# Block transposes on VectorE for the last seven head pairs, and another order of scores and masks in the first batch

## The chip, the core and the metric

The kernel runs on one core of one Trainium2 chip. The engines of a core run side by side, each through its own queue in order: TensorE (PE, matmuls and transposes by an identity), VectorE (DVE), ScalarE (ACT), GpSimd (POOL) and SyncE (SP, which here only issues DMAs). The metric is the device time in microseconds of one launch, the median of several runs.

## What is computed

Two blocks follow each other: block-sparse attention over 4 batches, 8 heads, 768 positions and a head size of 64, and then a Fourier mixing block with a two-layer network over rows of 512.

```python
scores = scale * np.matmul(q, k.transpose(0, 1, 3, 2))
# mask: block window, first and last block, three sampled blocks of 32 per block row
scores = np.where(mask, scores, -1000000000.0)
attn = np.exp(scores - np.max(scores, axis=-1, keepdims=True))
attn = attn / (np.sum(attn, axis=-1, keepdims=True) + 1e-09)
x = np.matmul(attn, v).transpose(0, 2, 1, 3).reshape(B, S, H * D)

u = x + np.real(np.fft.fft(np.fft.fft(x, axis=1), axis=2))
un = (u - mean(u)) / np.sqrt(var(u) + 1e-06)
return u + np.maximum(un @ w_ch1, 0.0) @ w_ch2
```

## The kernel before

Two heads make a pair, and there are 16 pairs, numbered n, four to a batch. A pair needs q and k with the head's 64 features along the partitions: `turned[n, 0]` (qT) and `turned[n, 1]` (kT), each 128 partitions (two heads of 64) by 768 positions. The positions of q are not in their natural order but in the one that the Fourier part wants (`_ORDER`); those of k stand six to a partition of the load, so that a tile of 128 keys holds every sixth position.

`load_q` and `load_k` bring q and k in by DMA with positions on the partitions, in pieces of 256 bytes. `turn(n, a, half)` (L433 to L464) turns one half: three or four TensorE transposes of 128 by 128 into a PSUM bank (L447), then for k one ScalarE copy (L450), for q nine small copies in all (L456) that put the positions in order. After the second half a ScalarE square with a running sum (L462) keeps a bound on the scores, which at the end decides whether a slower general path (`general`) has to run; with these inputs it does not.

The main loop is `slot(sl)` (L1177). A slot is two units, and a unit is 128 keys by 384 queries of both heads; six slots make a pair, 24 a batch or phase, and 96 all of it. In a slot come the scores of its two units (`scores`, L470), their exp (`weigh`, L488), then the products with v of the slot before (`values`, L512). In phase 0 the mask is added to the scores by TensorE, as a second, bf16 product of two small matrices of 24 rows (`of_k`, `off_q`, L483), and the exp goes straight to the tile `e`; row sums are matmuls as well (`add_up`, L569). From phase 1 on, VectorE multiplies the exp by a mask of bytes (L499), and GpSimd adds up the sums (L509). Score banks in PSUM are two, one for each unit of a slot.

In between stands work that a planner places: it keeps, while the program is built, a model of when each engine will be free (`busy`, `when`, `free`). Short things wait in the list `short`: a turn of the next pair, `place` (L532, transposes the attention's output back, "xt" in the profile), `total` (L575), `mask_step` (L317). `gap` issues what the model says is ready. At the end of a slot a loop (L1238) issues what is left. Turns of pair n + 1 are put on the list in slots 1, 2 (q) and 4, 5 (k) of pair n; pairs 9 to 15 are turned while pairs 8 to 14 are worked on, in phases 2 and 3. The mixing block of a batch (`mixer`: the Fourier products, `quad` with line L898 and L903, `channels` with L954 and L957) runs in the phases after its own, as steps of the list `late` between attention slots, and for the last batch after the loop.

Also in phase 0, 32 chunks of the two weight matrices, which come as pairs of 32-bit words, are rounded to fp32 (`w_round`, L404): two ScalarE and five VectorE operations a chunk, 1.42 chunks a slot. `w_load` fills six rooms for them.

Before the loop, `turn(0, 1, 0)` and `turn(0, 0, 0)` turn the first halves of pair 0, `warm` issues matmuls whose result is not used, and VectorE builds the mask's matrices (`spread_k`, `spread_q`, `twice`). For the first turn of q the copies alternate between VectorE and ScalarE.

Of the kernel before, what the change touches and what calls it, by code (L numbers as in the profile page):

```python
# [11 lines left out]
FP32 = mybir.dt.float32  # L12
# [6 lines left out]
ACT = mybir.ActivationFunctionType  # L19
# [45 lines left out]
           ((384, 64, 191, 64, 64, -1), (704, -128, 64, 63, 63, -1), (640, 127, 0, 1, 1, 1)))  # L65


def _rows(view, tile):

    got = []  # L70
    for t, p0, runs, jump, n, s0, step in _ORDER:
        if t != tile:
            continue
        at = view[s0:s0 + 1, :]
        row, col = list(at.ap[0])[0], list(at.ap[1])
        if jump > 0:
            got.append((p0, runs * n, bass.AP(tensor=at.tensor, offset=at.offset,
                                              ap=[[jump * row, runs], [step * row, n], col])))
            continue
        for r in range(runs):  # L80
            at = view[s0 + r * jump:s0 + r * jump + 1, :]
            got.append((p0 + r * n, n, bass.AP(tensor=at.tensor, offset=at.offset,
                                               ap=[[step * row, n], col])))
    return got
# [3 lines left out]
def kernel(  # L88
# [14 lines left out]
    nc = tc.nc  # L103

    B, H, S, D = q.shape
    DM = H * D
    FF = w_ch1.shape[1]
    P = 128
    C = S // P
    BLK = 32  # L110
    NB = S // BLK
    NR = sampled_blocks.shape[1]
    HS = S // 2
# [7 lines left out]
    scale = 1.0 / float(D) ** 0.5  # L121
    KA = D + NB
    NP = H // 2
    LIMIT = 400.0

    const = ctx.enter_context(tc.tile_pool(name="const", bufs=1))

# [25 lines left out]
    peaks = const.tile([P, 2 * B * NP], FP32, name="peaks")  # L153

    ld = ctx.enter_context(tc.tile_pool(name="ld", bufs=1))
    ldv = ctx.enter_context(tc.tile_pool(name="ldv", bufs=2))
    tp_p = ctx.enter_context(tc.tile_pool(name="tp_p", bufs=2))
# [9 lines left out]
    ps_s = ctx.enter_context(tc.tile_pool(name="ps_s", bufs=2, space=PSUM))  # L167
# [6 lines left out]
    when = {"PE": 0.0, "ACT": 0.0, "DVE": 0.0, "POOL": 0.0}  # L174
    free = {"m": [0.0, 0.0], "t": [0.0]}

    def busy(engine, us, after=0.0):
        when[engine] = max(when[engine], after) + us
        return when[engine]
# [11 lines left out]
    HOP = 0.1  # L191

    pairs = [(b, j) for b in range(B) for j in range(NP)]
    loaded, v_of = {}, {}

    def load_k(n, queue=None):

        b, j = pairs[n]
        kt = loaded.get((n, 1))
        if kt is None:  # L200
            kt = ld.tile([P, C, 2, D], FP32, tag="k", name="kr")
        for i in range(2):
            (queue or nc.sync).dma_start(out=kt[:, :, i, :],
                                         in_=k[b, 2 * j + i].rearrange("(p c) d -> p c d", p=P))
        loaded[n, 1] = kt

    def load_q(n):

        b, j = pairs[n]
        qt = loaded.get((n, 0))  # L210
        if qt is None:
            qt = loaded[n, 0] = ld.tile([P, T, 2, 2, D], FP32, tag="q", name="qr")
        for t in range(T):
            for i in range(2):
                rows = q[b, 2 * j + i][2 * P * t:2 * P * (t + 1), :]
                nc.sync.dma_start(out=qt[:, t, :, i, :],
                                  in_=rows.rearrange("(p r) d -> p r d", r=2))
# [36 lines left out]
    def bit(n):  # L254
# [5 lines left out]
                      in_=bass.AP(tensor=_words(sampled_blocks, NB * NR), offset=0,  # L260
                                  ap=[[0, NB], [1, 2 * NB * NR]]))
# [3 lines left out]
    def warm(n):  # L265

        m = ps_m.tile([P, P], FP32, tag="m", name="warm")
        for _ in range(n):
            nc.tensor.matmul(m, ident, ident, start=True, stop=True)
# [4 lines left out]
                         func=ACT.Exp)  # L274
# [15 lines left out]
    at_k = acc_p.tile([P, 2, 2 * HS], BF16, tag="acc", name="at_k")  # L290
    at_q = acc_p.tile([P, 2, 2 * HS], BF16, tag="acc", name="at_q")
    of_k, off_q, keep_q = at_k[:, 0, :], at_q[:, 0, :], at_q[:, 1, :]

    def twice(t):
        nc.vector.tensor_copy(out=t[D:D + NB, :], in_=t[0:NB, :])
# [3 lines left out]
    kb = bit(1)  # L299
# [86 lines left out]
    for w, w_sb in ((w_ch1, w1_sb), (w_ch2, w2_sb)):  # L386
        rows, cols = w.shape
        words = _words(w, rows * cols)
        for row in range(rows // P):
            for col in range(0, cols, WN):  # L390
                src = bass.AP(tensor=words, offset=2 * (row * P * cols + col),
                              ap=[[2 * cols, P], [1, 2 * WN]])
# [37 lines left out]
    turned, e_of, acc_of, o_of, sums_of, x_of, sp_of = {}, {}, {}, {}, {}, {}, {}  # L430
    s_at, e_at, oT_at, acc_at = {}, {}, {}, {}

    def turn(n, a, half):  # L433

        t = loaded[n, a]
        if half == 0:
            turned[n, a] = tp_p.tile([P, S], FP32, tag="qk"[a] + "T", name="qk"[a] + "T")
        dst = turned[n, a]
        first = n == 0 and half == 0
        tag, pool = ("m", ps_m) if first and a == 0 else ("t", ps_t)  # L440
        tp, at = pool.tile([P, 512], FP32, tag=tag, name="tp"), bank(tag)
        if a == 0:
            parts = [t[:, c // 2, c % 2, :, :] for c in (range(4, 6) if half else range(4))]
        else:
            parts = [t[:, T * half + c, :, :] for c in range(T)]
        for c, part in enumerate(parts):
            nc.tensor.transpose(tp[:, c * P:(c + 1) * P], part, ident)  # L447
        done = busy("PE", 0.15 * len(parts)) + HOP
        if a == 1:
            nc.scalar.copy(out=dst[:, half * HS:(half + 1) * HS], in_=tp[:, 0:HS])  # L450
            give(at, busy("ACT", 0.5, done))
        else:
            for i, (to, to_jump, frm, jump, cnt, step) in enumerate(_TURNED[half]):
                on, copy = (("DVE", nc.vector.tensor_copy) if n == 0 and (half == 1 or i % 2 == 0)
                            else ("ACT", nc.scalar.copy))
                copy(out=_grid(dst, to, 2, to_jump, cnt, 1),  # L456
                     in_=_grid(tp, frm, 2, jump, cnt, step))
                end = busy(on, 0.27 if cnt > 1 else 0.18, done)
            give(at, end)
        if half == 1:  # L460
            flat = t.rearrange("p t r i d -> p (t r i d)" if a == 0 else "p c i d -> p (c i d)")
            nc.scalar.activation(out=flat, in_=flat, func=ACT.Square,  # L462
                                 accum_out=peaks[:, 2 * n + a:2 * n + a + 1])
            busy("ACT", 1.05)  # L464

    UP = 2 * C
    UNITS = len(pairs) * UP
    SLOT = 2

    def scores(u):  # L470
        n, w = divmod(u, UP)
        half, c = divmod(w, C)
        qT, kT = turned[n, 0], turned[n, 1]
        s = ps_s.tile([P, 2, 512], FP32, tag="s", name="s")
        busy("PE", 0.72 if n >= NP else 1.0, max(e_at.get(u - SLOT, 0.0), z_at[u % 2]))
        s_at[u] = when["PE"] + HOP
        for i in range(2):
            nc.tensor.matmul(s[:, i, 0:HS], kT[D * i:D * i + D, c * P:(c + 1) * P],  # L478
                             qT[D * i:D * i + D, half * HS:(half + 1) * HS],
                             start=True, stop=n >= NP)  # L480
        if n < NP:
            for i in range(2):
                nc.tensor.matmul(s[:, i, 0:HS], of_k[D * i:D * i + NB, c * P:(c + 1) * P],  # L483
                                 off_q[D * i:D * i + NB, half * HS:(half + 1) * HS],
                                 start=False, stop=True)
        return s

    def weigh(u, s):  # L488
        n, w = divmod(u, UP)
        half, c = divmod(w, C)  # L490
# [313 lines left out]
    z_at = [0.0, 0.0]  # L804
# [287 lines left out]
    LEAVES = 9.0  # L1092
    SP = UP // SLOT
    SB = SP * NP
    W_PACE = 1.42
    short, apart, late = deque(), deque(), deque()
# [80 lines left out]
    def slot(sl):  # L1177
        phase, r = divmod(sl, SB)
        n, s = divmod(sl, SP)
        units = range(SLOT * sl, SLOT * sl + SLOT)  # L1180
        if sl < B * SB:
            for u, ps in [(u, scores(u)) for u in units]:
                weigh(u, ps)
        if not late:
            gap(1.5)
# [10 lines left out]
        if sl > 0 and s == (5 if reuse else 3) and sl <= B * SB:  # L1196
            b, j = pairs[n]
            at = oT_at[n, 0]
            if reuse:
                until(lambda: (b - 2, 0) in finished)  # L1200
                at = when["PE"] + LEAVES
# [3 lines left out]
        if sl < B * SB and n % NP == 1 and s == 1:  # L1205
            b = pairs[n - 1][0]
            at = oT_at[n - 1, 1]
            if b >= 2:
                until(lambda: (b - 2, 1) in finished)
                at = when["PE"] + LEAVES  # L1210
# [1 line left out]
        if sl > SB and s == 0 and sl <= B * SB:  # L1212
            short.append(("t", acc_at[n - 1, 1], lambda: total(n - 1)))
        if n + 1 < len(pairs):
            for at, a, half in ((1, 0, 0), (2, 0, 1), (4, 1, 0), (5, 1, 1)):
                if s == at:
                    short.append(("t", 0.0, lambda a=a, half=half: turn(n + 1, a, half)))
            if s == 1:
                load_v(n + 1)
# [9 lines left out]
        us = sum(step[1] for step in late)  # L1229
# [5 lines left out]
            channel_step()  # L1235
            gap(max(state["owed"], 0.0))

        while short and (s in (2, 5) or len(short) > 1 or phase == 0 or sl == B * SB):  # L1238
            short.popleft()[2]()
        if s == 3 and n + 2 < len(pairs):  # L1240
            load_q(n + 2)
        if s == 0 and 0 < n < len(pairs) - 1:
# [6 lines left out]
    def highest():  # L1249
# [7 lines left out]
        flag = sm.tile([1, 1], I32, tag="flag", name="flag")  # L1257
        nc.vector.tensor_scalar(out=flag, in0=top, scalar1=LIMIT, scalar2=None, op0=ALU.is_gt)
        return flag
# [9 lines left out]
    state["got"] = 2  # L1269
    turn(0, 1, 0)  # L1270
    turn(0, 0, 0)
    warm(3)
    spread_q(keep_q[0:NB, :], keep)
    w_loads()
    for sl in range(B * SB + 1):
# [112 lines left out]
```

## Time and profile before

| what | before |
|---|---|
| median of 11 runs | 1109.5 us (1108.31 to 1113.95) |
| the profiled execution | 1109.49 us, of which the span of its instructions is 1107.7 us |
| VectorE busy | 663.9 us, 60% of the span |
| transposes for q and k on TensorE (L447) | 192, of them 84 for pairs 9 to 15 |
| scores (L478), all records | 160.3 us busy |
| mask products of phase 0 (L483) | 96 records, 16.1 us busy |
| clock granted to TensorE, mean | 0.994 of full |

The profile is one execution on the chip. An operation is named by its line, its output and inputs and their sizes. A TensorE matmul in fp32 shows as two records, and matmuls are pipelined: the time from one start to the next is what a matmul costs its queue, and the duration of a record is longer than that. The attention's slots of phase 0 lie from 9.2 to 133 us, those of phase 1 to 248, phase 2 to 574, and phase 3 to about 825; then the last batch is mixed to the end.

### The profile page before, as it was taken

To read this page: it belongs to the slowest core of one execution; us is meant where nothing else is said; L and a number is where in the kernel's file an instruction comes from. 1 tells how busy PE (TensorE), PEld (TensorE's weight loads), DVE (VectorE), ACT (ScalarE), POOL (GpSimd) and SP (SyncE) were. 2 spreads that over 40 slices of the span, in tenths; PEclk is the share of its full clock that TensorE was granted. 3 is DMA by queue.
4 is the path that set the end of the run, shared out by engine and by line. 5 is a ranking of instruction groups with operands and counts; after the bars stand their busy time and mean duration, and the time that the engine had idled before them with its cause. 6 is when DMAs were issued, how large, how long until landed. Compare 5 with 4: busy or idle time off the path is not lost.

```text
span 1107.7 us, 12468 instructions
## 1 busy us (share of the span) xinstructions
PE 1067.3 (96%) x4446; PEld 545.2 (49%) x4446; DVE 663.9 (60%) x1216; ACT 393.5 (36%) x818; POOL 274.0 (25%) x302
## 2 busy tenths in 40 slices
PE   8999988998899999999999999999999999999996
PEld 4333333544455545444444555454444555568675
DVE  5888878497754525653458355544356446575563
ACT  6788755555112102253443212244330202120210
POOL 1000078688100001255537000344440001000000
PEclk9999999999999999999999999999999999999998
DMA  7756311011000000210110000211000000100001
GB/s 219 209 176 214 95 45 49 15 45 43 0 1 1 0 1 24 63 40 18 43 29 15 1 0 1 52 49 29 1 1 0 1 1 20 38 1 1 1 16 44
DMA packets 65187, 44.30 MB, mean 40 GB/s; under 512 B 52814, under 2 KB 57948, under 8 KB 65116
## 3 DMA queue, kind: packets, MB, share of 16 engines
q1 hardware_dynamic: 63228, 42.62, 13.7%
q10 hardware_dynamic: 1856, 0.79, 0.3%
q8 instruction: 37, 0.61, 0.2%
q14 instruction: 34, 0.28, 0.1%
q0 software_dynamic: 32, 0.01, 0.0%
HBM read 37.11 MB, written 6.29 MB: 39 GB/s over the span
## 4 chain that ended last, share of the span: by engine, by line
PE 87%; DVE 8%; ACT 3%; issue 2%; POOL 0%; ACTq 0%; DVEq 0%; POOLq 0%
PE y L954 23%; PE z L898 15%; PE s L478 11%; PE o L522 9%; PE yp L898 7%; PE yy L1017 6%; PE xp L898 4%; DVE e L499 2%; PE tp L447 2%; PE zp L711 1%; PE sp L569 1%; PE xt L540 1%; PE zp L682 1%; PE s L483 1%; PE utp L823 1%
## 5 line engine op out<-in xcount | busy, mean ns | idle before, releaser
L509 POOL TENSOR_TENSOR acc<-acc,e 128x384 f32<-128x384 f32 x192 | 198.2, 1065 | 91.5 <-DVE e L499 91.0
L499 DVE TENSOR_TENSOR e<-s,mask 128x768 f32<-128x768 f32 x144 | 131.0, 950 | 77.2 <-ACT s L497 76.8
L478 PE MATMUL s<-qT,kT 64*128 64x384 f32 x768 | 160.3, 522 | 7.6 <-DVE e L499 7.1
L522 PE MATMUL o<-e,vr 128*64 128x384 f32 x768 | 145.8, 501 | 0.0
L497 ACT ACTIVATE s<-s 128x768 f32<-128x768 f32 x144 | 109.2, 795 | 63.5 <-PE s L478 60.5
L957 DVE TENSOR_TENSOR x<-y,x 128x512 f32<-128x512 f32 x72 | 49.7, 690 | 134.0 <-PE y L954 133.9
L954 PE MATMUL y<-w_sb,hB 128*128 128x512 f32 x288 | 128.4, 595 | 1.1 <-DVE x L957 1.0
L954 PE MATMUL y<-w_sb,hA 128*128 128x512 f32 x288 | 128.8, 594 | 0.6 <-ACT zs L713 0.6
L509 POOL TENSOR_TENSOR acc<-e 128x384 f32<-128x384 f32 x48 | 51.7, 1098 | 228.9 <-DVE e L499 173.5
L903 DVE TENSOR_TENSOR hA<-z,hA 128x384 f32<-128x384 f32 x64 | 35.7, 557 | 111.0 <-PE z L898 111.0
L478 PEld LDWEIGHTS s<-qT,kT 64*128 64x128 f32 x768 | 62.5, 186 | 67.0 <-DVE e L499 24.7
L898 PE MATMUL z<-unT,t 128*128 128x384 f32 x256 | 93.0, 486 | 0.0
L774 POOL TENSOR_SCALAR st<-st 128x1 f32<-128x1 f32 x24 | 6.6, 275 | 344.6 <-DVE st L773 344.2
L954 PEld LDWEIGHTS y<-w_sb,hB 128*128 128x128 f32 x288 | 53.3, 190 | 64.7 <-issue 62.1
L522 PEld LDWEIGHTS o<-e,vr 128*64 128x64 f32 x768 | 46.9, 137 | 74.4 <-issue 71.7
L954 PEld LDWEIGHTS y<-w_sb,hA 128*128 128x128 f32 x288 | 52.9, 190 | 59.5 <-issue 56.5
L907 ACT ACTIVATE hA<-hA 128x384 f32<-128x384 f32 x64 | 33.4, 522 | 123.2 <-DVE hA L903 122.6
L898 PEld LDWEIGHTS z<-unT,t 128*128 128x128 f32 x256 | 48.7, 190 | 34.0 <-issue 0.2
L907 ACT ACTIVATE hB<-hB 128x384 f32<-128x384 f32 x64 | 33.5, 523 | 86.3 <-DVE hB L903 86.3
L898 PE MATMUL z<-t,w_sb 128*128 128x384 f32 x128 | 47.5, 495 | 3.1 <-DVE t L860 3.1
L898 PE MATMUL xp<-unT,w_sb 128*128 128x384 f32 x128 | 47.2, 491 | 1.5 <-ACT zs L713 1.1
L898 PE MATMUL z<-t,t 128*128 128x384 f32 x128 | 47.4, 493 | 0.0
(190 smaller groups left out, 1395.4 us busy)
## 6 DMA issues: line engine op xcount, KB each, us to landing
wraw<-in_moe_w_ch_dram SPq DMA_DIRECT2D x32, 512.0 KB
qr<-in_q_dram SPq DMA_DIRECT2D x90, 64.0 KB
vr<-in_v_dram SPq DMA_DIRECT2D x30, 192.0 KB
kr<-in_k_dram SPq DMA_DIRECT2D x28, 192.0 KB
out_dram<-x SPq DMA_DIRECT2D x16, 128.0 KB
out_dram<-x SPq DMA_DIRECT2D x8, 256.0 KB
out_dram<-x SPq DMA_DIRECT2D x8, 126.0 KB
out_dram<-x SPq DMA_DIRECT2D x4, 252.0 KB
```

The lines of the kernel that those rows point to most:

```text
L447: nc.tensor.transpose(tp[:, c * P:(c + 1) * P], part, ident)
L478: nc.tensor.matmul(s[:, i, 0:HS], kT[D * i:D * i + D, c * P:(c + 1) * P], qT[D * i:D * i + D, half * HS:(half + 1) * HS], start=True, stop ...
L497: nc.scalar.activation(out=s[:, :, 0:HS], in_=s[:, :, 0:HS], func=ACT.Exp, scale=scale)
L499: nc.vector.tensor_tensor(out=e, in0=s[:, :, 0:HS], in1=m.broadcast_to([P, 2, HS]), op=ALU.mult)
L509: nc.gpsimd.tensor_add(out=acc, in0=e_of[u - 1][:, i, :] if c == 1 else acc, in1=e[:, i, :])
L522: nc.tensor.matmul(o[D * i:D * i + D, :], vt[:, i, c, :], e[:, i, :], start=(c == 0), stop=(c == C - 1))
L898: nc.tensor.matmul(to, a[:, k, :], c[:, k, :], start=(k == 0), stop=(k == ND // 2 - 1))
L903: tt(out=to, in0=ps, in1=a, op=ALU.add)
L907: nc.scalar.activation(out=h, in_=h, func=ACT.Relu)
L954: nc.tensor.matmul(y, hs[0, half][:, l, m * P:(m + 1) * P], w2_sb[:, 4 * r + l, :], start=(l == 0), stop=(l == 3))
L957: nc.vector.tensor_tensor(out=x[:, m, :], in0=y, in1=x[:, m, :], op=ALU.add)
L1017: nc.tensor.matmul(ps, a[:, k, :], c[k // 2][:, k % 2, :] if isinstance(c, list) else c[:, k, :], start=(k == 0), stop=(k == 3))
```

## The change

Pairs 9 to 15 (`BY_VECTOR`) are loaded and turned in another way. `load_blocks` issues four DMAs a tensor, each of 32 partitions, in pieces of 128 bytes: partition 64 i + 32 g + r holds, for head i and feature group g, row r of every block of 32 positions. `flip_blocks` then transposes all 32 by 32 blocks of the tile in one VectorE instruction, q in place, and k into kT with an output pattern that spreads neighbouring positions over the six tiles. `in_order` copies q on ScalarE, in six copies, into the order that is wanted. `squares` is the sum for the bound, on its own; `LIMIT` goes from 400 to 200, as a partition's sum now holds half the features of a position. These five steps are issued at the end of slots 0, 1, 2, 4 and 5 of the pair before.

In phase 0 `scores` takes both units of a slot: first both units' score products, then both units' mask products. The mask's matrices are now used with 64 rows, of which those over 24 are zero from two memsets.

The loop at the end of a slot takes what the model holds ready first, and stops when nothing is ready, but in slots 2 and 5, in the first slot of a phase and in the first two slots of all. The second half of q of pair 1 is turned in slot 3, not 2. All copies of the first half of q of pair 0 are on ScalarE, and `warm(3)` after the first turns becomes `warm(7)`.

```diff
-    LIMIT = 400.0
+    LIMIT = 200.0
...
+    BY_VECTOR = 2 * NP + 1
+
+    def load_blocks(n, a, tile):
+        b, j = pairs[n]
+        for i in range(2):
+            rows = (q, k)[a][b, 2 * j + i].rearrange("(t r) (g d) -> g r t d", r=BLK, d=BLK)
+            for g in range(D // BLK):
+                p0 = D * i + BLK * g
+                nc.sync.dma_start(
+                    out=tile[p0:p0 + BLK, :].rearrange("r (t d) -> r t d", d=BLK), in_=rows[g])
+        loaded[n, a] = tile
...
+    nc.vector.memset(of_k, 0.0)
+    nc.vector.memset(off_q, 0.0)
...
-                on, copy = (("DVE", nc.vector.tensor_copy) if n == 0 and (half == 1 or i % 2 == 0)
+                on, copy = (("DVE", nc.vector.tensor_copy) if n == 0 and half == 1
                             else ("ACT", nc.scalar.copy))
...
+    def flip_blocks(n, a):
+        t = loaded[n, a]
+        out = t
+        if a == 1:
+            kT = turned[n, 1] = tp_p.tile([P, S], FP32, tag="kT", name="kT")
+            out = _at(kT, 0, [(1, P), (P, C)])
+        nc.vector.transpose(out=out, in_=t)
+        busy("DVE", 1.0)
+
+    def in_order(n):
+        t = loaded[n, 0]
+        qT = turned[n, 0]
+        for to, frm, *dims in _IN_ORDER:
+            nc.scalar.copy(out=_at(qT, to, [(d[0], d[2]) for d in dims]),
+                           in_=_at(t, frm, [(d[1], d[2]) for d in dims]))
+        busy("ACT", 1.7, when["DVE"])
...
+        for u in us:
+            c = u % C
+            s = ps_s.tile([P, 2, 512], FP32, tag="s", name="s")
+            got.append((u, s))
             for i in range(2):
-                nc.tensor.matmul(s[:, i, 0:HS], of_k[D * i:D * i + NB, c * P:(c + 1) * P],
-                                 off_q[D * i:D * i + NB, half * HS:(half + 1) * HS],
+                rows = slice(D * i, D * i + D)
+                nc.tensor.matmul(s[:, i, 0:HS], kT[rows, c * P:(c + 1) * P], qT[rows, queries],
+                                 start=True, stop=n >= NP)
+        for u, s in got if n < NP else ():
+            for i in range(2):
+                rows = slice(D * i, D * i + D)
+                nc.tensor.matmul(s[:, i, 0:HS], of_k[rows, c * P:(c + 1) * P], off_q[rows, queries],
                                  start=False, stop=True)
...
-        while short and (s in (2, 5) or len(short) > 1 or phase == 0 or sl == B * SB):
-            short.popleft()[2]()
+        while short and (s in (2, 5) or len(short) > 1 or phase == 0 or r == 0):
+            ready = [i for i in short if max(i[1], min(free[i[0]])) <= when["PE"] + 0.1]
+            if not ready and s not in (2, 5) and r > 0 and sl > 1:
+                break
+            item = ready[0] if ready else short[0]
+            short.remove(item)
+            item[2]()
+        if BY_VECTOR <= n + 1 < len(pairs):
+            for at, fn, args in ((0, squares, (n + 1, 0)), (1, flip_blocks, (n + 1, 0)),
+                                 (2, in_order, (n + 1,)), (4, flip_blocks, (n + 1, 1)),
+                                 (5, squares, (n + 1, 1))):
+                if s == at:
+                    fn(*args)
...
-    warm(3)
+    warm(7)
```

## The prediction

> **What bounds the kernel now.** I read the shares by engine first, then the slices over time, then the groups of TensorE instructions by form, then what TensorE waited for, then short stretches of the timeline, and last the busy time of all engines by stage. From the page, busy time and two rows of the forty slices:
>
> ```profile
> PE 1067.3 (96%) x4446; PEld 545.2 (49%) x4446; DVE 663.9 (60%) x1216; ACT 393.5 (36%) x818; POOL 274.0 (25%) x302
> PE   8999988998899999999999999999999999999996
> DVE  5888878497754525653458355544356446575563
> ```
>
> TensorE (PE) is busy nearly all the time, in every stage. A busy share alone would not prove it, since ends of matmuls are modelled; so the waits of TensorE's queue, whose rows are: who waited for whom, total us, times, longest:
>
> ```profile
> PE s L478 <- DVE e L499: 7.1, 9, 2.2
> PE xt L540 <- ACT oT L528: 4.1, 5, 1.0
> PE tp L447 <- ACT qT L456: 3.4, 3, 1.1
> ```
>
> These are the largest; all waits together are about 31 us of 1107.7. So nearly every microsecond of matmul issue that goes is a microsecond of time, unless another engine then ends last. The reader is to see also that VectorE's (DVE) slices read 8 early on: that stage has a second limit close by.
>
> Phase 0 (batch 0, the first 24 slots of two units), from the timeline of TensorE (start, us, line, shapes, count):
>
> ```profile
> 38.58 0.92 PE L478 MATMUL s<-qT,kT 64*128 64x384 f32 x4
> 39.43 0.33 PE L483 MATMUL s<-at_q,at_k 24*128 24x384 bf16 x2
> 39.70 0.92 PE L478 MATMUL s<-qT,kT 64*128 64x384 f32 x4
> 40.54 0.34 PE L483 MATMUL s<-at_q,at_k 24*128 24x384 bf16 x2
> 40.81 1.51 PE L522 MATMUL o<-e,vr 128*64 128x384 f32 x8
> ```
>
> Scores, mask, scores, mask: 40.81 - 38.58 = 2.23 us a slot. A later stage, where a pair is turned by TensorE and scores have no mask product:
>
> ```profile
> 542.08 0.60 PE L447 MATMUL tp<-ident,qr 128*128 128x128 f32 x4
> 542.61 1.56 PE L478 MATMUL s<-qT,kT 64*128 64x384 f32 x8
> 544.10 1.51 PE L522 MATMUL o<-e,vr 128*64 128x384 f32 x8
> 545.54 0.44 PE L447 MATMUL tp<-ident,qr 128*128 128x128 f32 x2
> 545.91 1.56 PE L478 MATMUL s<-qT,kT 64*128 64x384 f32 x8
> 547.40 1.51 PE L522 MATMUL o<-e,vr 128*64 128x384 f32 x8
> ```
>
> Two units' scores side by side take 544.10 - 542.61 = 1.49 us, and a turn of four blocks holds the queue 0.53 us, of two 0.37, with no gap. Busy time by stage (stretch, us, then PE, PEld, DVE, ACT, POOL busy, clock, DMA share, GB/s):
>
> ```profile
> 71.00:133.00 62.00, 60.02 (x376) 21.15 (x376) 53.81 (x124) 49.85 (x101) 0.00 (x0) 1.00 0.60 187
> 446.00:574.00 128.00, 127.41 (x546) 59.66 (x544) 64.83 (x94) 54.42 (x115) 58.58 (x60) 1.00 0.15 38
> 701.00:825.00 124.00, 123.08 (x524) 56.09 (x524) 62.16 (x90) 49.52 (x98) 55.24 (x57) 1.00 0.09 25
> ```
>
> Where the turns go away (446 to 825) VectorE is half free and ScalarE (ACT) more; in phase 0 VectorE is at 53.81/62 = 87%, ScalarE at 80%.
>
> [...] the trace's own 128x768 product (L499) takes 950[...]. [...] The trace's nearest is a strided read, at_k<-wide over 768 elements in steps of six floats: 0.84 us[...]; a write in steps of 512 bytes it doesn't show. [...] score matmuls follow each other in 0.32 us, score to mask (64*128 to 24*128) in 0.415, so some 0.09 us a change.
>
> **Part by part**, against the profiled execution: span 1107.7, 1109.5 with what lies around it, which is also the median.
>
> A. *Turns of pairs 9 to 15.* Gone: 7 x 12 = 84 transposes. I summed, from the timeline, each turn from its first start to the next other matmul's start, after 250 us: 13.4 us in 26 blocks, of which 1.9 us are two waits in them (1.1 for the bank of the turn before it at 262.4, 0.7 at 700.5). Taken: -13.4. Added on VectorE: 14 flips. The q flip, in place, 0.96 us; the k flip writes in steps of 512 bytes: [...] I take 1.3. Together 16 us beside 64.8 + 62.2 busy in 252: hidden on VectorE itself. But VectorE runs in order, and behind a flip stand the e products (L499), which free the score banks. In a slot with only scores and values (732.5 to 735.5) the products end at 736.3, 0.85 us into the next slot, and the next product can start at 1.75: the hole is 0.9 us, and the flip of 0.96 to 1.3 just overfills it; in longer slots it is wide. 14 x about 0.15 = +2, from 0 to +14 (a whole us each). ScalarE: nine copies of 0.16 to 0.28 (2.2 us) and two of 0.48 go, six copies from SBUF come, some 1.8 us by the rows' fixed part; the squares stay. Less work, no cost. The loads: 3072 pieces of 128 bytes a tensor in place of 1536 of 256; a 256-byte packet takes 18 ns on one of 16 engines, so the pieces take 2 to 4 us, SP's issue of four DMAs 3 to 5, as now (six issues, 4.1). They are asked for three (q) or four (k) slots ahead, at least 10 us: hidden; if not, the flip waits and everything on VectorE with it (the last rival). q's load on SP still waits for the last reader of its tile, now the ordering copies, one slot before, so nothing behind it on SP moves. Net -11.4.
>
> B. *Scores of both units, then both masks.* Slot now 2.23. After: 1.49 for the scores with the change to the next mode, then two mask products, 0.16 and 0.26 = 1.91; if the zero-padded 64-row masks count as the same mode, 0.09 less, 1.82. So 0.32 to 0.40 x 24; I take 0.30, leaving 0.02 for waits: -7.2, at best -9.6, and nothing if the exp chain ends last. The exp waits till after the second unit's scores, by 0.5 us; covered, since values and sums (1.5 + 0.85) come between, and the banks are wanted over 2 us later.
>
> C. *The order of what fills gaps.* What isn't ready no longer stops the queue, unless the slot is 2 or 5. The waits of xt (L540) in phase 0 are 0.8, 1.0, 1.0, in phase 1 1.3 and 0.6. About half goes: -2 (0 to -4).
>
> D. *Start.* The q copies of the first half all on ScalarE: 6 in 1.0 us (as at 17.0) where hand-overs between two engines took 1.6; scores could start at 8.5 in place of 9.17. But four more warm-ups: the six records issue 0.21 us apart until 8.4; fourteen would end near 10.3 at this pace, or 9.5 if the clock rises at 8.7 as the trace has it. +0.5 (-0.5 to +1.2). Two memsets of 768 bf16, 0.3 to 0.9 us each, push VectorE's chain to the mask (now done at 7.97, wanted at 10): hidden.
>
> E. *What is late next.* Phase 0 rests on VectorE's rounding of the weights, 32 x 2.92 us: its waits for more of it are 13.2 us in all, so the stage can't shrink by more without VectorE ending last. B, C and D ask for 8. Already at 133 the first product (137.06) waits for the last rounding. I charge +2 (0 to +8).
>
> Sum: -11.4 - 7.2 - 2 + 0.5 + 2 = -18.1. Span 1089.6, time **1091.4, said as 1091**.
>
> **Rivals.**
> 1. *VectorE becomes the bound of phase 0* (E at +8): for it 87% and the late product at 137.06; against it 13 us of waits to use up. 1109.5 - 18.1 + 6 = 1097.
> 2. *Everything lands*: [...] flips wholly in holes (-2), E at nothing (-2): 1085. For it the half-free VectorE.
> 3. *The turns' room is not given back*: TensorE waits out the same time for the products, since a slot of scores and values has only 0.3 us to spare at 735.5. A at nothing: 1103. Against it: slots of 3.0 us without a wait (732.5).
> 4. *The slower side: the flip at the head of VectorE's in-order queue.* If it is slow by its wide steps or waits for its 128-byte pieces, every product behind it is late, and TensorE with it. It decides from (18.1 + 2)/14 = 1.4 us of stall a flip; at 2.3 us a flip, 32 us, the time is 1109.5 - 20.1 + 32 = 1121. Against it the packet times and the 0.84 us strided read.
>
> **How the numbers follow.** Forecast 0.58 (own range 1087 to 1096), rival 1 0.14, rival 2 0.14, rival 3 0.06, rival 4 0.08. The range 1083 to 1101 takes in the forecast and rivals 1 and 2 with A's cost up to +12 and leaves out rivals 3 and 4. Within 0.2% is 2.2 us, about what this kernel's spread can tell: a weak form of rivals 3 and 4 together, 0.02. Slower 0.08, faster 0.90.
>
> **What would show it.** TensorE's transposes fall by 84; from 446 to 825 its waits stay below a few us; flips near 0.96 and 1.3 us; two scores and two masks in 1.8 to 1.9 us; the first values of phase 1 some 7 us earlier. Flips over 2 us, or scores waiting for e after them, would make A wrong; no idle VectorE in phase 0 and products late at its end would make E the cause; a first score later than 10 us D.

## The result, and the profile after

| | before | after |
|---|---|---|
| median of the runs, us | 1111.23 (1108.31 to 1117.12, 31 runs) | 1099.67 (1098.14 to 1100.83, 8 runs) |
| profiled execution, us | 1109.49 | 1100.62 |
| its span, us | 1107.7 | 1098.8 |

The ratio is 0.9897, with a 95% interval from 0.9881 to 0.9912. The time lies in the predicted range. The span fell by 8.9 us where the working had 18.1, so the direction was right and the sum was not. The medians are 11.6 us apart, because the execution profiled before lies 1.7 us below its median and the one after 1.0 us above its own.

The page of the kernel after, busy time and two rows of slices:

```profile
PE 1055.7 (96%) x4370; PEld 539.5 (49%) x4370; DVE 670.9 (61%) x1229; ACT 390.1 (35%) x786; POOL 271.0 (25%) x302
PE   8999988988999999999999999999999999999996
DVE  5899887598745524654567536554456346575563
```

TensorE lost 11.6 us of busy time and is as full as it was. Its waits (who waited for whom, total us, times, longest):

```profile
PE s L551 <- DVE e L574: 11.7, 10, 2.5
PE tp L486 <- ACT qT L495: 3.4, 3, 1.1
PE utp L898 <- DVE un L861: 3.1, 1, 3.1
```

The scores' wait for the e products grew from 7.1 to 11.7 us. The copies behind xt, second before with 4.1 us, are gone from the head of the list. A slot of phase 0, from TensorE's timeline (start, us, line, shapes, count):

```profile
66.54 1.56 PE L551 MATMUL s<-qT,kT 64*128 64x384 f32 x8
67.94 0.49 PE L559 MATMUL s<-at_q,at_k 64*128 64x384 bf16 x4
68.36 1.51 PE L597 MATMUL o<-e,vr 128*64 128x384 f32 x8
```

Scores and masks now take 68.36 - 66.54 = 1.82 us in place of 2.23. That was one of the two values I held possible: the first 64-row mask starts 0.316 us after the last score, like a score after a score, where the 24-row one started 0.415 us after it, and this in spite of another type. At the end of phase 0, from the timeline of all engines:

```profile
127.17 0.69 DVE L461 TENSOR_TENSOR w_sb<-w_sb,wraw 128x512 f32<-128x512 f32 x1
127.78 0.22 DVE L401 COPY sd_sb<-tab 128x127 f32<-128x127 f32 x1
127.92 0.22 DVE L402 COPY sd_sb<-tab 128x128 f32<-128x128 f32 x1
128.17 0.22 DVE L403 COPY sd_sb<-tab 1x128 f32<-1x128 f32 x1
128.31 1.80 DVE L574 TENSOR_TENSOR e<-s,mask 128x768 f32<-128x768 f32 x2
129.31 2.51 PE L551 MATMUL s<-qT,kT 64*128 64x384 f32 x8 [2.26 <-DVE e L574]
```

VectorE ends last: the last rounding, three table copies, then the first e products of phase 1, for which TensorE waits 2.26 us. In the kernel before the same scores waited 0.49 us:

```profile
138.06 1.78 PE L478 MATMUL s<-qT,kT 64*128 64x384 f32 x8 [0.49 <-DVE e L499]
```

And the eight score matmuls behind the wait after take 2.51 us, not 1.56. The busy time by stretch says why (stretch, us, then PE, PEld, DVE, ACT, POOL busy, granted clock, DMA share, GB/s):

```profile
126.81:130.22 3.41, 1.16 (x9) 0.35 (x7) 3.35 (x8) 0.48 (x1) 0.02 (x1) 1.00 0.55 161
130.22:133.63 3.41, 3.41 (x11) 1.22 (x12) 2.27 (x3) 1.59 (x2) 3.36 (x4) 0.50 0.00 0
181.42:184.83 3.41, 1.54 (x8) 0.60 (x8) 3.38 (x5) 0.58 (x1) 0.80 (x1) 1.00 0.38 115
184.83:188.25 3.41, 3.41 (x13) 1.27 (x11) 2.23 (x4) 1.49 (x3) 0.00 (x0) 0.50 0.00 0
724.14:727.55 3.41, 1.68 (x10) 0.49 (x8) 1.82 (x2) 2.39 (x6) 0.16 (x1) 1.00 0.55 89
727.55:730.97 3.41, 3.41 (x12) 0.95 (x11) 2.10 (x3) 1.50 (x2) 3.29 (x4) 0.50 0.17 26
...
71.00:133.00 62.00, 58.99 (x386) 23.48 (x388) 57.23 (x124) 50.32 (x101) 2.74 (x3) 0.98 0.59 179
...
446.00:574.00 128.00, 126.16 (x520) 56.42 (x520) 69.41 (x101) 53.24 (x100) 58.70 (x61) 1.00 0.18 37
701.00:825.00 124.00, 121.35 (x483) 54.45 (x481) 65.30 (x98) 45.99 (x83) 55.98 (x58) 0.99 0.10 23
```

In each of the first three pairs of lines TensorE is busy for less than half of the first, and the clock is 0.50 in the second. There are five such stretches of 3.41 us in the loop after (130.2, 184.8, 242.9, 270.2, 727.6) and two before (148.7, 281.8), of which this is the first:

```profile
145.20:148.70 3.50, 1.56 (x10) 1.05 (x12) 1.93 (x7) 1.45 (x10) 3.50 (x4) 0.99 0.00 0
148.70:152.10 3.40, 3.40 (x14) 1.22 (x12) 1.52 (x2) 2.37 (x5) 0.38 (x1) 0.50 0.21 48
```

Each puts off all later slots by some 1.65 us (1.4 to 1.8 at the four slots of fill, below). The prediction didn't have them. The last three lines of the longer list are the stages shown of before: from 71 to 133 us VectorE rose from 87 to 92% (57.23/62), though 10 us of phase 1 now lie in that window. From slot 12 to slot 24 it is busy for 52.73 of 56.25 us, 94%, where it was 54.11 of 62.30. From 446 to 825, where it took the flips, it is still half free.

### The profile page after: what moved, and what is told of

Read it like the earlier page. It is cut to its first block, busy times and chain, and to the rows that moved or that the text cites. A ratio compares the mean times of both kernels' runs of the same rounds, so it can differ in the third digit from the quotient of the medians.

```text
span 1098.8 us, 12275 instructions
## 1 busy us (share of the span) xinstructions
PE 1055.7 (96%) x4370; PEld 539.5 (49%) x4370; DVE 670.9 (61%) x1229; ACT 390.1 (35%) x786; POOL 271.0 (25%) x302
## 4 chain that ended last, share of the span: by engine, by line
PE 83%; DVE 10%; ACT 2%; issue 2%; DMA 1%; POOL 1%; ACTq 0%; DVEq 0%; POOLq 0%
PE y L1029 23%; PE z L973 15%; PE s L551 10%; PE o L597 8%; PE yp L973 7%; PE yy L1092 6%; PE xp L973 3%; DVE e L574 3%; PE zp L786 2%; PE zp L757 1%; PE sp L644 1%; DMA out_dram<-x 1%; PE xt L615 1%; PE tp L486 1%; DVE wraw L460 1%
## 5 line engine op out<-in xcount | busy, mean ns | idle before, releaser
L551 PE MATMUL s<-qT,kT 64*128 64x384 f32 x768 | 157.6, 523 | 13.5 <-DVE e L574 11.7
L597 PE MATMUL o<-e,vr 128*64 128x384 f32 x768 | 148.2, 508 | 0.0
L993 ACT COPY hA<-xp 128x384 f32<-128x384 f32 x32 | 15.3, 479 | 95.8 <-PE xp L973 95.8
```

What stands on the lines that cost most here:

```text
L551: nc.tensor.matmul(s[:, i, 0:HS], kT[rows, c * P:(c + 1) * P], qT[rows, queries], start=True, stop=n >= NP)
L597: nc.tensor.matmul(o[D * i:D * i + D, :], vt[:, i, c, :], e[:, i, :], start=(c == 0), stop=(c == C - 1))
```

## The experiments

"Slot" below is the start of a slot's first score in the profiled execution; 0 to 23 are phase 0, slot 54 begins pair 9. A difference between slots of two kernels shows where time is won or lost. The kernel before was run again beside each group: 1111.2 us (44 runs), 1109.75 (9) and 1109.55 (13) in the median. Its lowest times in the three groups are 1108.31, 1108.34 and 1108.36 us, so times of different groups are set side by side below.

### One part of the change at a time

**a_only**: the kernel before with the block transposes. The fillers run in the old order, but all of them in the first slot of a phase.

```diff
-    while short and (s in (2, 5) or len(short) > 1 or phase == 0 or sl == B * SB):
+    while short and (s in (2, 5) or len(short) > 1 or phase == 0 or r == 0):
         short.popleft()[2]()
+    if BY_VECTOR <= n + 1 < len(pairs):
+        ...
```

> Before with the block transposes alone (pairs 9 to 15), scores, masks, copies and warm-ups as before; the end-of-slot loop keeps its old order but also empties the list in the first slot of a phase. Theory (most of what is missing went to half-clock stretches and to exps that wait behind the ordering copies): TensorE's transposes fall by 84 and 11 to 12 us of its busy time go, 3 to 5 us come back as waits and half-clock stretches, so 6 to 8 us faster than before. The prediction's own term: 11.4 us faster. Rival (the flips hold up VectorE's queue and eat the gain): under 3 us faster, and waits for e right after flips.

Measured: 1106.38 us (20 runs), ratio 0.9961 (0.9949 to 0.9973). That is 4.8 us in the median, between the rival's under 3 and the 6 to 8 expected. In its profiled run TensorE's transposes are 11.4 us shorter, the span only 1.4: five stretches at half clock in place of two.

**b_only**: the kernel before with the scores of both units ahead of both masks, and the two memsets.

> Before with both units' scores ahead of both units' masks alone (with the two memsets). Theory (VectorE's rounding of the weights is what ends phase 0): a slot's scores and masks take 1.82 us in place of 2.22, so TensorE enters phase 1 about 9 us earlier, and gives 2 to 5 us back there waiting for the first products and at half clock: 4 to 7 us faster in all. Rival (the gain stays): 9 to 10 us faster.

Measured: 1104.02 us (9 runs), ratio 0.9931 (0.9909 to 0.9953). Scores and masks of the 24 slots take 43.9 us in place of 53.4, which is 9.5 less. Some 3 us of that went into waits (8.1 us up to slot 24, where the kernel before has 4.5, more than half of them for the copies behind xt). So slot 24 starts 6.6 us earlier; 5.4 us are left at the end.

**cd_only**: the kernel before with the other order of fillers, slot 3 for q's second turn, the first copies on ScalarE, and the warm-ups.

```diff
-    warm(3)
+    warm(7)
...
-            for at, a, half in ((1, 0, 0), (2, 0, 1), (4, 1, 0), (5, 1, 1)):
+            for at, a, half in ((1, 0, 0), (2 if n > 0 else 3, 0, 1), (4, 1, 0), (5, 1, 1)):
```

> Before with the other end-of-slot loop, the later turn in slot 3, the first copies on ScalarE and seven warm-ups alone. The prediction's terms: waits of xt go, 2 us, and the start costs 0.5: 1.5 us faster. Rival (the waits only move to other places): within 1 us of before.

Measured: 1109.82 us (20 runs), ratio 0.9983 (0.9972 to 0.9995). Slot 24 starts 3.1 us earlier, with the xt waits of phase 0 gone, and the last slot 1.0 us later: one stretch more at half clock (1.65 us), 1.0 us more at slot 25, and waits around slot 49 and in pairs 12 and 13. The median is 1.4 us lower, about what was expected.

The parts alone give 0.4, 0.7 and 0.2%, which is 1.3% together against 1.0% measured. In the profiled spans it is the other way round: 1.4, 5.4 and -1.0 us, 5.8 together against 8.9. A stretch more or less in a run is worth as much as either difference, so no interplay of the parts can be read from this.

### Is it the clock?

**fill**: the changed kernel with more work, idle matmuls ahead of the scores that wait.

```diff
+        if sl in (25, 37, 48, 82):
+            warm(8)
         if sl < B * SB:
             for u, ps in scores(units):
```

> The changed kernel with eight more unused matmuls ahead of the scores of slots 25, 37, 48 and 82, where TensorE waits 1.7 to 2.5 us in the changed kernel and its clock is granted at half for 3.4 us right after. Nothing else moves. Theory (these waits cost their length and then 1.7 us more in a half-clock stretch): up to four stretches go, 3 to 7 us faster than the changed kernel though TensorE has more to do, and the waits for e are filled. Rival (the waits alone cost, the clock does not matter): equal to the changed kernel or up to 2 us slower.

Measured: 1094.95 us (4 runs, 1094.82 to 1095.07), ratio 0.9849 (0.9812 to 0.9885). That is 4.7 us under the changed kernel with some 8 us more of TensorE work. Four stretches are gone, one is left (267.7). The slots show it in steps: 1.6 us at each of slots 26 and 38, 1.8 at slot 83 and 1.4 at slot 49. So the stretches are a cost of their own, and where TensorE's idle time was filled, four of five did not come.

### Where the idle time comes from

**early**: the changed kernel with each chunk of weights rounded one slot earlier.

```diff
-        while state["w"] < min(len(wchunks), W_PACE * sl):
+        while state["w"] < min(len(wchunks), W_PACE * sl + 1):
```

> The changed kernel with each chunk of weights rounded one slot earlier (the first in slot 0), nothing else. Theory (VectorE's roundings and table copies end last at the change from phase 0 to phase 1, and TensorE's 2.26 us wait at 129.3 us with the 3.41 us of half clock after it come from that): the last rounding ends some 3 us earlier (near 125 instead of 127.9 us), the wait at 129.3 falls below 0.7 us, the half-clock stretch at 130.2 is gone, and the run is 2 to 4 us shorter than the changed kernel's (about 1096 us). Rival (the roundings are not what is late; TensorE's own work fills phase 0): the first products of phase 1 start where they started, within 0.5 us, and the time stays at 1099.7 us within 1 us. Against the theory also: roundings earlier wait for their chunks' loads, and the wait is only moved to slots 1 to 5.

Measured: 1095.24 us (5 runs), ratio 0.9859 (0.9839 to 0.9879): 4.4 us under the changed kernel. Its timeline at the same place:

```profile
124.30 0.69 DVE L461 TENSOR_TENSOR w_sb<-w_sb,wraw 128x512 f32<-128x512 f32 x1
125.44 1.80 DVE L574 TENSOR_TENSOR e<-s,mask 128x768 f32<-128x768 f32 x2
127.05 1.56 PE L551 MATMUL s<-qT,kT 64*128 64x384 f32 x8
```

The products start 2.9 us earlier, the wait is gone, and so is the half clock: the eight matmuls take 1.56 us. Slots 25 and 26 win 2.3 and 1.9 us, the wait and its stretch. The theory held, and here it can be seen that the two are one cost of about 4 us.

**held**: the changed kernel with the squares, flips and ordering copies issued behind the next slot's exponentials.

```diff
-                    fn(*args)
+                    held.append((fn, args))
...
+        for fn, args in held:
+            fn(*args)
+        held.clear()
```

> The changed kernel with the steps of the last seven pairs that ScalarE and VectorE do alone (the squares, the two block transposes and the six ordering copies) issued after the next slot's exponentials and products instead of at the end of the slot before; the same work in another place of the queues. Theory (the ordering copies stand on ScalarE ahead of an exponential that is due, so that at pair 9's beginning TensorE waits 1.73 us at 726.5 us and runs 3.41 us at half clock after it): the wait there falls below 0.6 us, the stretch at 727.6 is gone, and the time falls by 1.5 to 4 us, to some 1097 us. Rival (the place in the queues doesn't matter, the slots of phase 3 have room for it): no stretch changes and the time stays within 1 us of 1099.7. If the later issue makes the flips or copies late for the pair's first scores, waits of over 1 us appear at the start of pairs 9 to 15 and the time rises.

Measured: 1100.68 us (5 runs), ratio 0.9918 (0.9898 to 0.9937). A miss: the wait grew to 2.67 us. Outputs on SP's queue went out 2.1 us later (701.25 in place of 699.16, and those behind them), as the addition into x on VectorE that they wait for ended 2.1 us later, and the copy into the x tile on ScalarE waited 3.66 us for the transfer (0.46 after). Moving everything moved too much.

**both**: early and held together.

> The two edits together: weights rounded a slot earlier, and the steps of the last seven pairs behind the next slot's exponentials. If the two waits with their half-clock stretches are separate costs, the gains add up: 4 to 7 us under the changed kernel, some 1094 us, with three stretches instead of five. If a stretch that is avoided only lets another wait set one off later (the rival), the number of stretches stays at four or five and the time above 1097 us.

Measured: 1095.79 us (5 runs), ratio 0.9873 (0.9852 to 0.9893), the gain of early alone. Its trace has five stretches, as the rival said, though the time stayed below the rival's 1097.

**first**: the changed kernel with only the six ordering copies moved, and forward, to the head of the same slot.

```diff
+        if s == 2 and BY_VECTOR <= n + 1 < len(pairs):
+            in_order(n + 1)
         if not late:
             gap(1.5)
...
-                                 (2, in_order, (n + 1,)), (4, flip_blocks, (n + 1, 1)),
+                                 (4, flip_blocks, (n + 1, 1)),
```

> The changed kernel with the six ordering copies of q issued at the head of the pair's third slot (right behind its exponentials) instead of at its end, behind the copy into the x tile; nothing else. Theory (at pair 9's beginning the copy into x waits for an output's transfer, the ordering copies stand behind it and delay the exponentials by their 1.87 us): the exponentials at 724.6 us start near 722.8, the 1.73 us wait of the scores falls below 0.4 us, the half-clock stretch at 727.6 is gone, and the time falls by 1.7 to 3.4 us, to 1096 to 1098 us. Rival (it is the transfer alone that is late, as in the kernel that held the steps back, whose wait grew to 2.67 us with the copies out of the way): the wait stays above 1.3 us and the time within 1 us of 1099.7.

Measured: 1099.15 us (4 runs), ratio 0.9903 (0.9888 to 0.9917). ScalarE's timeline of the changed kernel at pair 13:

```profile
721.11 0.48 ACT L616 COPY x<-xt 128x384 f32<-128x384 f32 x1 [0.46 <-DMA out_dram<-x]
721.49 0.53 ACT L982 ACTIVATE hA<-hA 128x384 f32<-128x384 f32 x1
722.39 0.52 ACT L982 ACTIVATE hB<-hB 128x384 f32<-128x384 f32 x1 [0.38 <-DVE hB L978]
722.82 1.87 ACT L528 COPY qT<-qb 128x256 f32<-128x256 f32 x6
724.60 1.49 ACT L572 ACTIVATE s<-s 128x768 f32<-128x768 f32 x2
```

and of this one, whose slots lie some 1.5 us later there:

```profile
723.86 0.52 ACT L982 ACTIVATE hB<-hB 128x384 f32<-128x384 f32 x1 [0.32 <-DVE hB L978]
724.29 1.49 ACT L572 ACTIVATE s<-s 128x768 f32<-128x768 f32 x2
```

Without 1.87 us of copies between them, the exponentials follow at once. The scores' wait of 1.73 us is gone and its stretch with it: 3.4 us between pair 13's fourth and sixth slot. (The expectations place this wait at pair 9's beginning; it is in pair 13.) Two other runs show the same 3.4 us, at slots 82 and 83: a_only has them and the kernel before has not, and no_a, further down, is without them. But 2.3 us were lost between slots 53 and 54, where the transposes of the first mixer waited a second time, and a further stretch followed. The timelines of GpSimd, VectorE and TensorE there:

```profile
267.34 4.03 POOL L584 TENSOR_TENSOR acc<-acc,e 128x384 f32<-128x384 f32 x4
271.76 0.57 POOL L851 TENSOR_TENSOR st<-st,neg_half 128x1 f32<-128x1 f32 x1
272.36 0.55 DVE L861 TENSOR_SCALAR un<-x,st 128x512 f32<-128x512 f32 x1 [2.80 <-POOL st L851]
273.05 1.09 PE L898 MATMUL utp<-ident,un 128*128 128x128 f32 x4 [2.32 <-DVE un L861]
```

TensorE waits for VectorE, which waits 2.80 us for a small step of the normalization on GpSimd, and that step stands behind 4.03 us of GpSimd's row sums. VectorE's wait is 2.80 us in held and both too, 2.79 in best below, and 0.7 us in the changed kernel, a_only, fill and early: of the kernels with block transposes, the four that move these copies have the long wait. Why their planner issues the step later, no run here shows. So the time is the one that the rival named, and the trace the one that the theory named.

### What is each worth without the clock?

**no_a**: the changed kernel without the block transposes.

```diff
-    BY_VECTOR = 2 * NP + 1
+    BY_VECTOR = B * NP
```

> The changed kernel without its block transposes: q and k of all sixteen pairs are turned by TensorE; the order of scores and masks, the memsets, the loop and the first loads stay as changed. Theory (from the kernel of before with the block transposes alone, which was about 5 us faster in the median and 1.4 us in its profiled span, and from the half-clock stretch that follows the 1.73 us wait at pair 9): the block transposes are worth 2 to 6 us inside the change, so this takes 1102 to 1106 us. Rival (the prediction's own figure of 11.4 us holds inside the change): 1109 to 1111 us, as much as before the change. Third (they are worth nothing once the stretch is paid): within 1 us of 1099.7.

Measured: 1105.32 us (5 runs), ratio 0.9952 (0.9932 to 0.9971), as the theory had it. So the transposes on VectorE are worth 5.6 us inside the change. What they free is seen on TensorE, around the third slot of pair 10, in its timeline. Without the block transposes:

```profile
499.49 0.60 PE L486 MATMUL tp<-ident,qr 128*128 128x128 f32 x4
500.02 1.56 PE L551 MATMUL s<-qT,kT 64*128 64x384 f32 x8
501.51 1.51 PE L597 MATMUL o<-e,vr 128*64 128x384 f32 x8
502.95 0.44 PE L486 MATMUL tp<-ident,qr 128*128 128x128 f32 x2
```

and in the changed kernel:

```profile
494.61 1.45 PE L1029 MATMUL y<-w_sb,hA 128*128 128x512 f32 x3
495.99 1.56 PE L551 MATMUL s<-qT,kT 64*128 64x384 f32 x8
```

The last y matmul stands before the scores now, and its step to them is 0.522 us where its step to the transposes was 0.429; the last of four transposes had 0.202 where the others had 0.11. The 0.09 us goes with the change of shape (128*128 to 64*128), and it stays. Over pair 10, with no wait in either kernel, in us of TensorE from start to start:

```
12 transposes        1.57 -> 0
40 y matmuls        17.56 -> 17.96   +0.40
48 scores            9.02 ->  9.24   +0.22
 8 sums              0.78 ->  0.85   +0.07
pair 10             38.39 -> 37.50   -0.89
```

So 0.9 of 1.6 us is kept.

**best**: early, first, and smaller fillers (1.05 us) where waits were left.

```diff
+        if sl in (37, 48):
+            warm(4)
...
+            if b == 0 and (half, m) == (0, 1):
+                warm(8)
             tp = pool.tile([P, ND, P], FP32, tag=tag, name="utp")
```

> The changed kernel with weights rounded a slot earlier, the ordering copies at the head of the slot, and idle matmuls put where TensorE still waits: four ahead of the scores of slots 37 and 48 (some 1.05 us each time, half of what the fillers of the earlier run took) and eight ahead of the transposes that waited 3.1 us at 270.6. Theory ([...] every one avoided is worth 1.65 us): the idle time of each such window falls below 1.6 us, no stretch is left between the start and the last output, and the run takes 1086 to 1089 us. Rival (length of the wait alone doesn't decide, or the fillers delay what they stand before): one or more stretches stay, 1090 us or more.

Measured: 1093.42 us (5 runs), ratio 0.9851 (0.9839 to 0.9864): faster than both kernels, but over the 1086 to 1089 us expected; the rival held. The small fillers did their work (the waits at slots 37 and 48 fell to 1.40 and 1.28 us, with no stretch behind). The third one was run at 259.2, ahead of other transposes than the ones that waited. The theory's windows are the 3.413 us into which "What sets a stretch off" divides the traces, and not all fell below 1.6 us of idle time: in the first of the lines below TensorE is busy for 0.63 us of 3.40. The second wait described under first is there too (2.71 us at 267.0), and two stretches are left:

```profile
262.50:265.90 3.40, 0.63 (x4) 0.42 (x4) 1.02 (x1) 0.90 (x2) 3.23 (x5) 1.00 0.00 0
265.90:269.30 3.40, 2.29 (x7) 1.72 (x8) 2.95 (x5) 0.58 (x1) 0.38 (x1) 0.50 0.00 0
269.30:272.70 3.40, 3.40 (x7) 1.89 (x6) 1.52 (x5) 0.48 (x1) 0.00 (x0) 0.50 0.00 0
```

**best_no_a**: the same without the block transposes.

> The same kernel with its block transposes taken away (TensorE turns q and k of all pairs), so that what they are worth is seen with few half-clock stretches on either side. Theory (per pair of slots' traces 0.9 us stays of the 1.6 us of TensorE that a pair's transposes took[...]): 5 to 7.5 us slower than with them, 1092 to 1095 us. Rival (the prediction's term): 11.4 us slower, 1098 us or more.

Measured: 1097.66 us (5 runs), ratio 0.9893 (0.9878 to 0.9907), 4.2 us over best, without any half clock in its loop. From pair 9 to the end the block transposes win 5.6 us for six pairs, 0.94 each; in pair 8 they lose 2.0, with the two stretches above. So the figure is 4.2 as it stands. Without these two it would be at most some 7.5 (4.2 + 2 x 1.65), an estimate: TensorE also waited for 1.1 us in the first of them, so that one cost less.

**before_fill**: the kernel before with fillers at its own waits.

```diff
+        if sl in (36, 37, 48):
+            warm(4)
...
+        if (n, a, half) == (5, 0, 1):
+            warm(4)
...
+            if b == 0 and p == 0:
+                spare = ps_t.tile([P, 512], FP32, tag="t", name="spare")
+                for _ in range(8):
+                    nc.tensor.matmul(spare[:, 0:P], ident, ident, start=True, stop=True)
```

> The kernel of before with idle matmuls where it waits before its half-clock stretches: four ahead of the scores of slots 36, 37 and 48 and of q's second turn of pair 5, eight ahead of the product that waited 3.1 us at 281.3. Theory (two stretches of 1.65 us in its profiled run, two to four in most of its runs): no stretch left, 1103.5 to 1106 us, so that the change without the clock's part is worth some 12 us. Rival (before had nothing to gain from this, the stretches are not what its runs differ by): within 1.5 us of 1109.5.

Measured: 1106.69 us (7 runs), ratio 0.9977 (0.9967 to 0.9988), no stretch left in its trace, and just above the time expected. Against the changed kernel with fillers (1094.95) the change is worth 11.7 us, and some 13.4 if the one stretch left in that one is taken off.

### What sets a stretch off

All stretches of one trace start at whole multiples of 3.41333 us from the point where its record of full clock begins (exact to 0.0004 of a multiple, in all 14 traces; in the changed kernel the fifth starts 727.553 - 7.340 = 720.213 us after that, which is 211 times). I divided each trace into windows of this length and added up TensorE's recorded waits in each that ran at full clock, from the third window to the end of the loop:

```
idle in the window   windows   half clock in the next one
0 to 1.0 us            4248      0
1.0 to 1.7 us            86      0
1.7 to 1.85 us            4      2
1.85 to 3.0 us           35     35
```

In these traces 1.73 us was followed by a stretch twice, 1.73 and 1.78 us once each were not, and from 1.85 on every window was; what decides between 1.7 and 1.85 us is not shown. The wait's length alone doesn't decide. The wait of 1.73 us at pair 13 was followed by a stretch in the changed kernel and not in early, though it lay within one window in both:

```profile
719.54:722.95 3.41, 1.68 (x12) 0.66 (x12) 1.25 (x2) 3.07 (x8) 0.00 (x0) 1.00 0.28 47
722.95:726.37 3.42, 3.42 (x21) 1.19 (x19) 2.37 (x4) 1.59 (x2) 2.65 (x3) 1.00 0.43 68
```

And the kernel before waited 2.16 us at 248.4 without one: 1.37 us of it fell in one window, the rest in the next. In a_only, b_only and cd_only, where it came 1.6 us later or 6.9 and 1.1 us earlier, the same wait (2.16 to 2.17 us) lay within one window, and a stretch followed.

## Why the prediction was right, and where it was off

The mechanism was right: TensorE is the bound, and what leaves its queue leaves the time, in part. The terms, in us of span:

| term | forecast | measured | by |
|---|---|---|---|
| A, room of the turns | -13.4 | -7.6 | no_a to after, from slot 48: -4.2 without pair 13's stretch (1.6) and wait (1.7) |
| A, flips in front of e | +2 | +1.7 | the wait in pair 13 |
| B | -7.2 | -6.6 | b_only, slot 24 |
| C and D | -1.5 | -3.1 | cd_only, slot 24 |
| E | +2 | +1.8 | the wait at slot 25, 0.49 to 2.26 |
| the clock | none | +5.0 | three more stretches of 1.65 |
| sum | -18.1 | -8.8 | span: -8.9 |

The sum closes better than its parts are known: the first score alone came between 8.2 and 10.9 us in traces of kernels with the same start.

- **A failed in the size of its first term.** I summed each turn "from its first start to the next other matmul's start", and this step holds about 0.09 us for the change of shape behind the turn (0.202 us where the others had 0.11), which goes over to the matmul that now stands there (0.522 for 0.429). Of pair 10's 1.57 us 0.89 was kept. I had read the same 0.09 us in phase 0 for B (0.415 for 0.32); in A I left it out. The 1.9 us of waits within the turns were counted as gained, while other waits came, as at 569, where xt waits 1.42 us for the sums (0.85 in no_a). Rival 3, A at nothing, falls with the 5.6 us of no_a.
- **A's second term had about the right size and the wrong place.** Not 14 small delays by flips: one wait, by the ordering copies on ScalarE, which I had costed at nothing since ScalarE has less to do. It has less work, but six copies in a row of 1.87 us stand in its queue ahead of exponentials.
- **The flips themselves.** VectorE's groups by form (busy, mean ns, idle before):

```profile
L520 DVE STREAM_TRANSPOSE kT<-kb 128x768 f32<-128x768 f32 x7 | 10.7, 1524 | 0.0
L520 DVE STREAM_TRANSPOSE qb<-qb 128x768 f32<-128x768 f32 x7 | 6.8, 968 | 0.0
```

  0.97 us for q, close to the 0.96 that I had estimated (a product of the same size, L499, takes 950 ns in the trace of before), and 1.52 for k where I took 1.3, my estimate too. No flip waited for its load. Rival 4 fell on both counts.
- **B came out by two errors that offset each other.** With the masks 0.316 us behind the scores instead of 0.415 a slot won 0.41 us where I took 0.30 (rival 2 had put 2.4 us in all on this), and some 3 us of the sum went into waits where I allowed 0.5. That -6.6 is close to -7.2 is luck in this. **C and D were low**: the waits of xt in phase 0 went altogether, and the first score came 0.5 us earlier rather than later, which is within its spread. In cd_only all of it was given back later.
- **E was right as a wait.** VectorE ends last at 128.3. Its price was doubled by the stretch behind it.
- **The clock was the missing term.** "if the clock rises at 8.7 as the trace has it" was all that the prediction had of it, for the start. I had read waits of 31 us in sum, and they are 33.3 after. But they were gathered otherwise: five windows with 1.73 to 2.66 us of them were followed by a stretch, where before it were two (1.90 and 2.90 us), and so TensorE ran 17.1 us at half clock where it had run 6.8. Rival 1's time, 1097, was nearest, for another reason: early shows that VectorE's part is about 4 us, wait and stretch together, and not the bound of the whole phase. That the time lies in the range at all is in part luck: the range reached up to 1101 for a late VectorE and costly flips, and it was the 0.09 us steps and 5 us of clock that used it up.

What stays open: why, with the ordering copies moved, the normalization step comes behind GpSimd's sums, and how low the time gets when its fillers stand where it waits. No run had the change without any stretch.

## What to carry to other kernels

On an engine that is full, count what a removed step leaves behind: here the 0.09 us at a change of shape went over to the neighbour, and only 0.9 of 1.6 us was kept. Look at the granted clock in stretches around the waits, before and after: the wait of 2.26 us on TensorE at slot 25 cost about 4, and a change that shortens one stage shifts later waits against the windows (the 2.16 us wait at 248.4 had no stretch behind it, and had one when it came 1.6 us later or 6.9 us earlier). Where a wait can't be taken away, a filler of 1 us ahead of it was worth 1.4 to 1.6 us (slots 37 and 48, best against early, where waits of 1.40 and 1.28 us were left).

## What the runs showed of the hardware that was not expected

- Half-clock stretches came in whole windows of 3.413 us, on one grid per run, after a window with TensorE idle for 1.85 us or more every time (35 of 35), and twice after 1.73 us; each cost some 1.65 us. A second stretch in a row came after windows at half clock with only 0.9 to 1.1 us of recorded idle time in two cases (early, best) and with 2.3 us in three.
- The kernel before ran at 1108.3 to 1117.1 us, its profiled run with two stretches and its version with fillers at 1106.64 to 1108.23. The spread between runs of one program goes with the clock: the mean granted clock was 0.995 to 0.997 in the ten runs of the kernel before, of the 66 beside the experiments, that took under 1108.5 us, and 0.986 to 0.988 in the three over 1116. That fits stretches that one run has and another has not, but only one execution of each was traced.
- A block transpose of 128x768 fp32 took 0.97 us with contiguous writes and 1.52 us with writes in steps of 512 bytes.
- The bf16 matmuls of 64 rows followed the fp32 matmuls of 64 rows after 0.316 us; those of 24 rows had come after 0.415, some 0.09 us more.
